# Second expert layer with the weights loaded and the hidden rows moving

## The chip, the cores and the metric

The kernel runs on one core of one Trainium2 chip. The metric is the device time of one execution in microseconds; lower is better. One further execution was profiled, and every row below comes from it.

## What is computed

Eight sequences of 2496 rows go through an attention without a softmax, and its 19968 result rows go through a mixture of eight experts. Each expert takes exactly 2496 rows, chosen greedily by the sorted gate logits.

```python
attn = np.maximum(scale * z @ z.T, 0.0) ** 2        # per sequence, z: 2496 x 64
x = (u * (attn @ v)).reshape(19968, 256)
# greedy by sorted logits x @ w_gate: token -> expert, 2496 rows each
for e in range(8):
    mask = assigned == e
    h = np.maximum(x[mask] @ w1[e], 0.0)            # 256 -> 1024
    out[mask] = h @ w2[e]                           # 1024 -> 256
```

All tensors are float32. Every float32 product is made of float32r parts: each operand is split into a high part (a copy rounded by ScalarE) and a low remainder (a subtraction on VectorE), and three products are summed: high by high, high by low, low by high.

## The kernel before

**Stages.** `attention` writes the rows x to a scratch tensor `xd` in HBM. `moe` then handles expert after expert (k), each in five groups (g) of rows: four of 512 and a last one of 448. A step n is one slice f of 128 of the 1024 hidden features of one group: 8 slices for a group, 40 steps for an expert, 320 in all. Beside the steps of one expert runs the routing of the next (`route`, a generator that `advance` drives in 88 units over 40 steps). It is a search for thresholds: VectorE makes masks (L124), TensorE counts them (L281, L405), VectorE picks the next interval, and at the end VectorE makes one-hot matrices (L523) which TensorE turns into row numbers (L529, L534).

**A group.** `gather_x` fetches 512 rows of `xd` by row number with four indirect DMAs of GpSimd's queue (L590). `tip_x` turns them on VectorE in blocks of 32 by 32 (L652), writes them with four DMAs of SyncE's queue to a scratch tensor `flat` (L655) and reads them back as features by rows (L658). `split_x` makes the high part on ScalarE (L665) and the low one on VectorE (L666). `layer1` multiplies w1 (loaded) by the turned rows (moving, six matmuls of 512 columns, L672 to L674), and makes the high part of the relu on ScalarE (L750) and the low part on VectorE (L752). In a group of 448 rows the low part of the last 64 rows goes to the free 64 columns of the high tile (L755).

**Second layer before.** For each of four blocks of 128 rows, `contract` loads the hidden block as weights and moves w2. The high and the low part of w2 lie side by side, so one matmul of 512 columns (L768) makes high by both, and one of 256 (L770) makes low by high. The last block of a group of 448 rows needs one matmul only (L765). Four PSUM banks, `y0` to `y3`, hold the result, already as rows. `put_y` adds the two halves (ScalarE copies one out, L792; VectorE adds the other, L793) and scatters the rows to the output with four indirect DMAs of GpSimd's queue (L801).

**Weights.** `load_w` loads an expert's w1 and w2 in four DMAs of SyncE's queue once the routing knows which expert comes next; `split_w` makes the two parts (ScalarE L618, VectorE L621). For w1 it reads every fourth element.

**Order.** A table (`at`) says at which step each part of a group is called, relative to the group's first step n0: gather at n0 - 12, `tip_x` at n0 - 8, `split_x` at n0 - 4, `put_y` at n0 + 7. `layer1` runs three steps ahead of `layer2`. Outside the parts that are written in a fixed order, a planner orders each engine's instructions by its own estimate of times; each engine then runs its list strictly in that order. `issue_after(x)` tells the planner that an instruction follows x on the same engine; `paced[-1]` is the low part (L752) made last. Of the eight PSUM banks, `hp` (result of layer 1) has two, `xp` and `srch` (routing) one each, `y0` to `y3` four.

Of the kernel before, what the change touches and what calls it, by code (L numbers as in the profile page):

```python
# [135 lines left out]
def moe(tc, xd, first, jp, identf, w1, w2, out, B, S, cp, dram):  # L136
# [18 lines left out]
    PLANS = ((4, 3, 3, 3, 3), (3, 3, 3, 3, 2, 2))  # L155
    ND = 15
    LA = 3
    AHEAD = 12
    LATE = 2
    YIELDS = 88  # L160
    with ExitStack() as ctx:
        rp = ctx.enter_context(tc.tile_pool(name="rp", bufs=1))
        wp = ctx.enter_context(tc.tile_pool(name="wp", bufs=3))
# [160 lines left out]
                with tc.issue_after(latest["mm"].ins):  # L324
                    nc.tensor.matmul(idle[:, :256], tri, oh[:, :32].rearrange("p j e -> p (j e)"), start=True, stop=True)  # L325

        paced = []

        def behind(lag):
            return tc.issue_after(paced[-lag].ins) if len(paced) >= lag else nullcontext()  # L330
# [253 lines left out]
        w1v = w1.rearrange("e (h p) (c f) -> e p c h f", c=2, p=128)  # L584
        w2v = w2.rearrange("e (c p q) d -> e p c q d", c=2, p=128)
        W1, W2, WR, XG, XT, XH, XL, HH, HL, HP, YP = {}, {}, {}, {}, {}, {}, {}, {}, {}, {}, {}
        scat = []

        def gather(dst, src, idx):
            return nc.gpsimd.indirect_dma_start(out=dst, out_offset=None, in_=src,  # L590
# [12 lines left out]
        def split_w(k, layer, c, half, parts="hl"):  # L603
            if half == 0 and "h" in parts:
                if layer == 1:
                    tiles = [wp.tile([128, 1024], F32R, name=f"w1{x}") for x in "hl"]
                    W1[k, c] = [t.rearrange("p (h q m) -> p h q m", h=DH, m=128) for t in tiles]
                else:
                    W2[k, c] = wp.tile([128, FT // 2, 2, D], F32R, name="w2")
            src = WR[k, layer, c]  # L610
            if layer == 1:
                src = src.rearrange("p (h m q) -> p h q m", h=DH, q=FT // 2)[:, half]
                h, l = [t[:, half] for t in W1[k, c]]
            else:
# [18 lines left out]
        def width(g):  # L633
            return min(512, S - 512 * g)

        def turn_x(k, g, ds):
            x = XG[k, g]
            w = width(g)
            t = [ps.tile([128, 512], F32, name=n, bufs=b) for n, b in (("xp", 1), ("hp", 2))]
            for d in ds:  # L640
                for i in range(4):
                    nc.tensor.transpose(t[d][:, i * 128:(i + 1) * 128], x[:, i, d * 128:(d + 1) * 128], identf)
            for d in ds:
                XH[k, g, d] = fp.tile([128, 512], F32R, name=f"xh{d}")[:, :w]
                XL[k, g, d] = fp.tile([128, 512], F32R, name=f"xl{d}")[:, :w]
                nc.scalar.activation(XH[k, g, d], t[d][:, :w], AF.Copy)
                nc.vector.tensor_sub(XL[k, g, d], t[d][:, :w], XH[k, g, d].bitcast(F32))

        def tip_x(k, g):
            tr = fp.tile([128, 2 * 4, 4, 32], F32, name="tr", bufs=1)  # L650
            with tc.issue_after(paced[-1].ins):
                nc.vector.transpose(tr.rearrange("p b t j -> p t b j"), XG[k, g].rearrange("p t d -> p (t d)"))  # L652
            flat = dram.tile([D, 512], F32, name="flat", bufs=2)
            for a in range(4):
                nc.sync.dma_start(flat[:, 128 * a:128 * a + 128].rearrange("(b i) n -> i b n", i=32),  # L655
                                  tr[32 * a:32 * a + 32].rearrange("i b t j -> i b (t j)"))
            XT[k, g] = fp.tile([128, DH, 512], F32, name="xt", bufs=1)
            nc.sync.dma_start(XT[k, g], flat.rearrange("(h p) n -> p h n", h=DH))  # L658

        def split_x(k, g):  # L660
            for d in range(DH):
                src = XT[k, g][:, d].rearrange("p (a t j) -> p t a j", a=4, t=4)
                hl = [fp.tile([128, 512], F32R, name=f"{n}{d}") for n in ("xh", "xl")]
                h, l = [t.rearrange("p (t a j) -> p t a j", t=4, a=4) for t in hl]
                nc.scalar.activation(h, src, AF.Copy)  # L665
                nc.vector.tensor_sub(l, src, h.bitcast(F32))  # L666
                XH[k, g, d], XL[k, g, d] = [t[:, :width(g)] for t in hl]

        def expand_part(k, g, f, p, c, d):
# [14 lines left out]
        def first_group():  # L684
# [11 lines left out]
            hp = [ps.tile([128, 512], F32, name=n, bufs=b) for n, b in (("hp", 2), ("hp", 2), ("y3", 1))]  # L696
# [43 lines left out]
        def layer1(k, g, f):  # L740
            w = width(g)
            if (k, g, f) in HP:
                p = HP.pop((k, g, f))
            else:
                p = ps.tile([128, 512], F32, name="hp", bufs=2)[:, :w]
                expand(k, g, f, p, slice(0, w))
            hh = fp.tile([128, 512], F32R, name="hh", bufs=LA + 1)
            h = hh[:, :w]
            l = fp.tile([128, 512], F32R, name="hl_", bufs=LA + 1)[:, :w]
            nc.scalar.activation(h, p, AF.Relu)  # L750
            n = w // 128 * 128
            paced.append(nc.vector.scalar_tensor_tensor(l[:, :n], p[:, :n], 0.0, h[:, :n].bitcast(F32),  # L752
                                                        op0=OP.max, op1=OP.subtract))
            if n < w:
                nc.vector.scalar_tensor_tensor(hh[:, w:w + w - n], p[:, n:], 0.0, h[:, n:].bitcast(F32),  # L755
                                               op0=OP.max, op1=OP.subtract)
            HH[k, g, f], HL[k, g, f] = hh, l
# [12 lines left out]
            nc.tensor.matmul(o[:, :D], l[:, c], w[:, 0], start=False, stop=(f == FT - 1), skip_group_check=True)  # L770

        def layer2(k, g, f):
            if f == 0:
                YP[k, g] = [ps.tile([128, 512], F32, name=f"y{i}", bufs=1) for i in range(4)]
            tail = FT - 1 - LA if (k, g) == (E - 1, NG - 1) else FT - 1
            if f < tail or tail == FT - 1:
                for i in range(4):
                    contract(k, g, f, i)
            elif f == FT - 1:
                for i in (3, 0, 1, 2):  # L780
                    for q in range(tail, FT):
                        contract(k, g, q, i)

        def put_y(k, g):
            y = fp.tile([128, 4, D], F32, name="y")
            idx = ROUTE[k]["idx"]
            w = width(g)
            order = (3, 0, 1, 2) if (k, g) == (E - 1, NG - 1) else range(4)
            for i in order:
                n = min(128, w - 128 * i)  # L790
                src = YP[k, g][i]
                nc.scalar.activation(y[:n, i], src[:n, D:], AF.Copy)  # L792
                nc.vector.tensor_add(y[:n, i], src[:n, :D], y[:n, i])  # L793
                if n < 128:
                    assert n == TL == 64
                    nc.vector.tensor_add(y[:n, i], src[TL:, :D], y[:n, i])
# [18 lines left out]
        for k in range(E):  # L815
            for g in range(NG):
                n0 = (k * NG + g) * FT
                if n0:
                    at(1 if (k, g) == (0, 1) else n0 - AHEAD + (LATE if (k, g) == (1, 0) else 0), gather_x, k, g)
                    if (k, g) == (0, 1):  # L820
                        at(n0 - 4, turn_x, k, g, range(DH))
                    else:
                        at(n0 - (7 if (k, g) == (1, 0) else 8), tip_x, k, g)
                        at(n0 - 4, split_x, k, g)
                at(n0 + FT - 1, put_y, k, g)
            n0 = k * PER
# [441 lines left out]
def _lay_out(inputs):  # L1268
# [16 lines left out]
    laid['moe_w1'] = _blocks(inputs['moe_w1'], 1)  # L1285
    return laid


# [20 lines left out]
```

## Time and profile before

| | us |
|---|---|
| median of 3 runs | 2434.04 (2432.58 to 2434.96) |
| time of the profiled execution | 2432.56 |
| its span, first to last instruction | 2430.5 |
| TensorE busy | 2380.0 |
| VectorE busy | 2068.5 |
| ScalarE busy | 1521.4 |
| GpSimd busy | 460.6 |
| mean granted clock of TensorE | 0.993 |

The span is 2.1 us shorter than the execution's time. Matmuls overlap in the records, so the distance from start to start tells their rate, and the duration does not. A granted clock of 1.0 is 2.4 GHz, 0.5 is 1.2 GHz; a stretch's figure is the mean. The attention ends at about 1370 us, the first expert's steps begin at about 1425 us, and the last routing ends at about 2200 us.

### The profile page before, as it was taken

Reading aid. Unit: us, or ns where it says so; the run is one execution under the profiler, and the core shown is the slowest. Engines: PE = TensorE matmul, PEld = TensorE weight load, DVE = VectorE, ACT = ScalarE, POOL = GpSimd, SP = SyncE. Lnnn points to the kernel's source line nnn. Section 1 sums busy time; section 2 is a strip of 40 time slices with the busy share of each in tenths; the row PEclk is TensorE's granted clock in tenths of the full one; section 3 lists DMA queues with packets and bytes.
Section 4 is the critical chain, followed back from the end, with each engine's and each line's share of the span. In section 5 each row is a group of like instructions: output and inputs, shape, how many; then the busy total and the mean of one; then the engine's idle time right before and its main releaser. Section 6 shows DMA issues by size and latency. Waiting matters only on the chain.

```text
span 2430.5 us, 42677 instructions
## 1 busy us (share of the span) xinstructions
PE 2380.0 (98%) x14724; PEld 1983.2 (82%) x14724; DVE 2068.5 (85%) x6220; ACT 1521.4 (63%) x2890; POOL 460.6 (19%) x690
## 2 busy tenths in 40 slices
PE   8999999999999999999999999899999999999998
PEld 6888888888888888888887787787888888888887
DVE  7898998998999998989989798979797979797443
ACT  7888888888888988888888223333332333333332
POOL 3020020020010200200100022333233333333332
PEclk9999999999999999999999999999999999999999
DMA  5153261261251532611511023232323323243331
GB/s 154 43 148 86 57 160 43 58 176 53 71 145 44 138 95 57 159 43 53 137 53 43 10 66 118 78 109 80 115 87 95 111 84 118 78 124 119 98 96 57
DMA packets 233848, 222.28 MB, mean 91 GB/s; under 512 B 95392, under 2 KB 192672, under 8 KB 233504
## 3 DMA queue, kind: packets, MB, share of 16 engines
q1 hardware_dynamic: 193088, 150.58, 21.3%
q0 software_dynamic: 40544, 68.98, 10.5%
q8 instruction: 116, 1.90, 0.3%
q14 instruction: 100, 0.82, 0.1%
HBM read 158.67 MB, written 60.82 MB: 90 GB/s over the span
## 4 chain that ended last, share of the span: by engine, by line
PE 82%; DVE 10%; issue 4%; POOL 1%; ACT 1%; DMA 1%; POOLq 0%; DVEq 0%; SPq 0%; ACTq 0%
PE acc L1038 41%; PE sc L996 11%; PE y L768 8%; PE hp L672 4%; PE hp L674 4%; PE hp L673 4%; PE y L770 4%; PE srch L281 2%; PE acc L1043 1%; POOL xg L590 1%; DVE mask L124 1%; DVE ob L523 1%; DVE w1l L621 1%; PE xp L325 1%; PE srch L529 1%
## 5 line engine op out<-in xcount | busy, mean ns | idle before, releaser
L1025 DVE TENSOR_TENSOR lo<-r,hi 128x512 fp32r<-128x512 f32 (+1 forms) x800 | 536.1, 673 | 83.1 <-ACT hi L1017 80.1
L1038 PE MATMUL acc<-hi,vh 128*128 128x512 f32 (+1 forms) x1520 | 590.8, 389 | 0.2 <-ACT vh L970 0.2
L1038 PE MATMUL acc<-lo,vh 128*128 128x512 f32 (+1 forms) x1520 | 587.7, 387 | 2.7 <-DVE lo L1025 2.7
L1038 PE MATMUL acc<-hi,vl 128*128 128x512 f32 (+1 forms) x1520 | 585.9, 385 | 0.0
L750 ACT ACTIVATE hh<-hp 128x512 fp32r<-128x512 f32 (+1 forms) x319 | 187.3, 587 | 629.9 <-PE hp L674 518.4
L1017 ACT ACTIVATE hi<-r 128x512 fp32r<-128x512 f32 (+1 forms) x780 | 500.2, 641 | 122.1 <-ACT r L1012 87.0
L1012 ACT ACTIVATE r<-r 128x512 f32<-128x512 f32 (+1 forms) x800 | 503.6, 639 | 2.5 <-DVE r L1006 2.4
L1079 DVE SCALAR_TENSOR_TENSOR lt<-xs,wgb 128x256 bf16<-128x256 f32 x1192 | 449.2, 417 | 0.0
L768 PE MATMUL y<-w,hh 128*128 128x512 f32 x1216 | 444.8, 399 | 0.7 <-DVE y L793 0.7
L1038 PEld LDWEIGHTS acc<-hi,vh 128*128 128x128 f32 x1520 | 286.2, 188 | 67.0 <-issue 13.8
L1008 ACT ACTIVATE r<-sc 128x512 f32<-128x512 f32 (+1 forms) x638 | 312.4, 614 | 40.3 <-PE sc L996 39.7
L1038 PEld LDWEIGHTS acc<-lo,vh 128*128 128x128 f32 x1520 | 286.3, 188 | 59.2 <-DVE lo L1025 8.2
L1038 PEld LDWEIGHTS acc<-hi,vl 128*128 128x128 f32 x1520 | 286.3, 188 | 52.1
L590 POOL DMA_INDIRECT xg<-xd,idx x160 | 181.2, 1133 | 513.3 <-DVE xg L628 281.1
L768 PEld LDWEIGHTS y<-w,hh 128*128 128x128 f32 x1216 | 229.0, 189 | 49.0 <-DVE y L793 2.2
L672 PE MATMUL hp<-xh,w1h 128*128 128x512 f32 (+2 forms) x642 | 256.5, 400 | 3.6 <-DVE hh L755 2.7
L673 PE MATMUL hp<-xl,w1h 128*128 128x512 f32 (+2 forms) x642 | 252.5, 393 | 1.2 <-DVE xl L666 1.1
L674 PE MATMUL hp<-xh,w1l 128*128 128x512 f32 (+2 forms) x642 | 250.6, 390 | 0.0
L996 PE MATMUL sc<-z,z 64*128 64x512 f32 (+1 forms) x1920 | 236.9, 389 | 4.2 <-ACT z L961 2.8
L996 PEld LDWEIGHTS sc<-z,z 64*128 64x128 f32 x1920 | 200.7, 185 | 31.2 <-ACT z L961 3.5
L959 POOL DMA_DIRECT2D z<-in_z_dram x35 | 18.7, 534 | 960.0 <-DVE lt L1079 530.0
L801 POOL DMA_INDIRECT out_dram<-y,idx x160 | 160.4, 1003 | 207.8 <-DVE y L793 120.9
(1193 smaller groups left out, 3152.1 us busy)
## 6 DMA issues: line engine op xcount, KB each, us to landing
ur<-in_u_dram SPq DMA_DIRECT2D x39, 512.0 KB
flat<-tr SPq DMA_DIRECT2D x152, 128.0 KB
xt<-flat SPq DMA_DIRECT2D x38, 512.0 KB
vh<-in_v_dram POOLq DMA_DIRECT2D x133, 128.0 KB
vr<-in_v_dram SPq DMA_DIRECT2D x32, 512.0 KB
xd<-tr SPq DMA_DIRECT2D x128, 128.0 KB
xs<-xd SPq DMA_DIRECT2D x32, 512.0 KB
wr<-in_moe_w_dram SPq DMA_DIRECT2D x32, 512.0 KB
```

The lines of the kernel that those rows point to most:

```text
L590: return nc.gpsimd.indirect_dma_start(out=dst, out_offset=None, in_=src, in_offset=bass.IndirectOffsetOnAxis(ap=idx, axis=0))
L672: nc.tensor.matmul(p[:, c], wh, xh, start=(d == 0), stop=False)
L673: nc.tensor.matmul(p[:, c], wh, xl, start=False, stop=False)
L674: latest["mm"] = nc.tensor.matmul(p[:, c], wl, xh, start=False, stop=(d == DH - 1))
L768: nc.tensor.matmul(o, h[:, c], w.rearrange("p s d -> p (s d)"), start=(f == 0), stop=(f == FT - 1), skip_group_check=True)
L996: nc.tensor.matmul(pair[s], key[b, p][r, c * 128:c * 128 + 128], query[b, g][r, :w], start=key is ZH and query is ZH, stop=key is ZL)
L1008: recent["r"] = nc.scalar.activation(r, p, AF.Relu, scale=scale)
L1012: nc.scalar.activation(R[n], R[n], AF.Square)
L1017: nc.scalar.activation(h, R[n], AF.Copy)
L1025: recent["l"] = nc.vector.tensor_sub(LO[n], a, h.bitcast(F32))
L1038: nc.tensor.matmul(o[d], w[:, c[d]], x, start=(kt == 0 and i == 0), stop=False)
L1079: nc.vector.scalar_tensor_tensor(t[r], src[r], 1.0, WG["rows"][r, e], op0=OP.mult, op1=OP.mult, accum_out=lg[r, j, e:e + 1])
```

## The change

The second layer exchanges its operands. w2 is loaded as weights and the hidden rows move, six matmuls of up to 512 columns for a slice (448 in a group of 448 rows). The result stands in two banks as features by rows, so it must be turned: VectorE turns each bank by blocks of 32 by 32 (`put_y`); three steps later `move_y` writes the blocks with four DMAs of SyncE's queue to a scratch tensor `rows` in HBM, in pieces of 64 floats, and reads them back as rows with one DMA (two in a group of 448); three more steps later `put_rows` scatters them. The very last group keeps the old way, with `xp` as one of its four banks.

The banks of the result rotate over three names (`YB`), and `hp` has three banks. Gather and `tip_x` come two steps sooner (`AHEAD` 14, `tip_x` at n0 - 10, `split_x` still at n0 - 4); since the routing's start is counted from `AHEAD`, it too starts and ends two steps sooner, except that `LATE` keeps expert 1's group 0 and the second start where they were. The turns of `tip_x` and `put_y` and the subtraction of `split_x` are collected in `before`, and the next L752 must follow them on VectorE. The low part of a 448-wide group is one instruction of 448 columns. Tiles `y` have one buffer instead of two, and so have the new tiles `yt`. On the host the columns of w1 are laid out so that `split_w` reads without a stride, and those of w2 so that the turned blocks give rows in order.

```diff
-    AHEAD = 12
-    LATE = 2
+    AHEAD = 14
+    LATE = 4
     YIELDS = 88
+    HPB = 3
+    YB = 3
...
             if layer == 1:
-                src = src.rearrange("p (h m q) -> p h q m", h=DH, q=FT // 2)[:, half]
+                src = src.rearrange("p (h q m) -> p h q m", h=DH, q=FT // 2)[:, half]
...
             with tc.issue_after(paced[-1].ins):
-                nc.vector.transpose(tr.rearrange("p b t j -> p t b j"), XG[k, g].rearrange("p t d -> p (t d)"))
+                before.append(nc.vector.transpose(tr.rearrange("p b t j -> p t b j"),
+                                                  XG[k, g].rearrange("p t d -> p (t d)")))
...
-                nc.vector.tensor_sub(l, src, h.bitcast(F32))
+                with tc.issue_after(paced[-1].ins):
+                    before.append(nc.vector.tensor_sub(l, src, h.bitcast(F32)))
...
-            n = w // 128 * 128
-            paced.append(nc.vector.scalar_tensor_tensor(l[:, :n], p[:, :n], 0.0, h[:, :n].bitcast(F32),
-                                                        op0=OP.max, op1=OP.subtract))
+            n = w // 128 * 128 if (k, g) == (E - 1, NG - 1) else w
+            with ExitStack() as turn:
+                while before:
+                    turn.enter_context(tc.issue_after(before.pop().ins))
+                paced.append(nc.vector.scalar_tensor_tensor(l[:, :n], p[:, :n], 0.0, h[:, :n].bitcast(F32),
+                                                            op0=OP.max, op1=OP.subtract))
...
         def layer2(k, g, f):
+            last = (k, g) == (E - 1, NG - 1)
             if f == 0:
-                YP[k, g] = [ps.tile([128, 512], F32, name=f"y{i}", bufs=1) for i in range(4)]
...
+                b = 2 * (k * NG + g)
+                names = [f"y{(b + d) % YB}" for d in range(DH)]
+                if last:
+                    names = names[:1] + ["xp"] + names[1:] + [f"y{(b + DH) % YB}"]
+                YP[k, g] = [ps.tile([128, 512], F32, name=n, bufs=1) for n in names]
+            if not last:
+                w = W2[k, f // 4][:, f % 4]
+                h, l = [t[k, g, f][:, :width(g)] for t in (HH, HL)]
+                for d in range(DH):
+                    c = slice(d * 128, d * 128 + 128)
+                    for i, (s, x) in enumerate(((0, h), (0, l), (1, h))):
+                        nc.tensor.matmul(YP[k, g][d][:, :width(g)], w[:, s, c], x, start=(f == 0 and i == 0),
+                                         stop=(f == FT - 1 and i == 2))
+                return
...
+            tr = fp.tile([128, 16, DH, 32], F32, name="yt", bufs=1)
+            with tc.issue_after(paced[-1].ins):
+                for d in range(DH):
+                    before.append(nc.vector.transpose(tr[:, :w // 32, d], YP[k, g][d][:, :w]))
+            YT[k, g] = tr
+
+        def move_y(k, g):
+            w = width(g)
+            tr = YT.pop((k, g))
+            rows = dram.tile([512, D], F32, name="rows", bufs=2)
+            dst = rows[:w].rearrange("(n i) d -> i n d", i=32)
+            for a in range(4):
+                nc.sync.dma_start(dst[:, :, 64 * a:64 * a + 64],
+                                  tr[32 * a:32 * a + 32, :w // 32].rearrange("i n h j -> i n (h j)"))
+            y = fp.tile([128, 4, D], F32, name="y", bufs=1)
+            n = w // 128
+            nc.sync.dma_start(y[:, :n], rows[:128 * n].rearrange("(t p) d -> p t d", p=128))
+            if n < 4:
+                nc.sync.dma_start(y[:w - 128 * n, n], rows[128 * n:w])
+            YT[k, g] = y
...
-                        at(n0 - (7 if (k, g) == (1, 0) else 8), tip_x, k, g)
+                        at(n0 - (7 if (k, g) == (1, 0) else 10), tip_x, k, g)
                         at(n0 - 4, split_x, k, g)
                 at(n0 + FT - 1, put_y, k, g)
+                if (k, g) != (E - 1, NG - 1):
+                    at(n0 + FT + 2, move_y, k, g)
+                    at(n0 + FT + 5, lambda k, g: put_rows(YT.pop((k, g)), k, g), k, g)
```

## Rows read from the trace of the kernel before

**Rows 1.** Busy time of each engine and its share of the span, from the page.

```profile
PE 2380.0 (98%) x14724; PEld 1983.2 (82%) x14724; DVE 2068.5 (85%) x6220; ACT 1521.4 (63%) x2890; POOL 460.6 (19%) x690
```

**Rows 2.** Stretches of the expert stage: length, busy per engine, clock, DMA share, GB/s.

```profile
1630.00:1680.00 50.00, 46.87 (x372) 39.55 (x371) 49.33 (x113) 19.11 (x35) 18.51 (x16) 1.00 0.37 120
1680.00:1756.00 76.00, 75.79 (x473) 62.56 (x473) 59.28 (x192) 22.81 (x45) 24.26 (x24) 0.98 0.29 83
1756.00:1806.00 50.00, 48.81 (x380) 41.35 (x380) 49.38 (x114) 19.66 (x35) 19.34 (x16) 1.00 0.39 124
...
2235.00:2415.00 180.00, 180.00 (x912) 153.11 (x910) 77.12 (x146) 59.43 (x118) 60.15 (x60) 1.00 0.30 88
```

**Rows 3.** TensorE's waits from 1500 to 2200 us: total, times, longest.

```profile
PE srch L281 <- DVE mask L124: 9.8, 5, 3.3
PE hp L672 <- DVE hh L755: 2.7, 1, 2.7
PE y L770 <- DVE hl__29448 L752: 2.0, 1, 2.0
PE srch L529 <- DVE ob L523: 1.9, 1, 1.9
```

**Rows 4.** TensorE's timeline, two blocks of 512-row groups: start, duration.

```profile
2264.58 0.39 PE L768 MATMUL y<-w,hh 128*128 128x512 f32 x1
...
2265.97 0.48 PE L672 MATMUL hp<-xh,w1h 128*128 128x512 f32 x1
...
2268.85 0.39 PE L672 MATMUL hp<-xh,w1h 128*128 128x512 f32 x1
...
2270.24 0.39 PE L768 MATMUL y<-w,hh 128*128 128x512 f32 x1
```

**Rows 5.** The same of the last 448-row group.

```profile
2405.64 0.37 PE L672 MATMUL hp<-xh,w1h 128*128 128x448 f32 x1
...
2406.86 0.39 PE L768 MATMUL y<-w,hh 128*128 128x512 f32 x1
...
2408.13 0.37 PE L672 MATMUL hp<-xh,w1h 128*128 128x448 f32 x1
```

**Rows 6.** VectorE's groups by line, 1600 to 2400 us: busy, mean ns of one.

```profile
L793 DVE TENSOR_TENSOR y<-y,y 128x256 f32<-128x256 f32 (+1 forms) x128 | 47.7, 415 | 0.0
...
L621 DVE TENSOR_TENSOR w1l<-wr,w1h 128x512 fp32r<-128x512 f32 x24 | 25.8, 1079 | 1.0 <-PE hp L674 1.0
...
L621 DVE TENSOR_TENSOR w<-wr,w 128x512 fp32r<-128x512 f32 x24 | 16.5, 690 | 0.6 <-ACT w L618 0.6
...
L755 DVE SCALAR_TENSOR_TENSOR hh<-hp,hh 128x64 fp32r<-128x64 f32 x48 | 10.2, 213 | 0.0
```

**Rows 7.** The attention's turn of a PSUM bank, group of the whole span by shape.

```profile
L1049 DVE STREAM_TRANSPOSE tr<-acc 128x512 f32<-128x512 f32 x64 | 41.8, 691 | 0.0
```

**Rows 8.** SyncE's queue in the attention: the turned rows written, then read back.

```profile
725.89 2.04 SPq L1062 DMA_DIRECT2D xd<-tr  x4
...
729.94 0.38 SPq L1066 DMA_DIRECT2D xs<-xd  x1
```

**Rows 9.** GpSimd's timeline, first and last scatter of one group, first of the last group.

```profile
2403.79 0.97 POOL L801 DMA_INDIRECT out_dram<-y,idx  x1 [17.16 <-DVE y L793]
...
2407.61 0.97 POOL L801 DMA_INDIRECT out_dram<-y,idx  x1 [0.30 <-issue]
2419.37 0.97 POOL L801 DMA_INDIRECT out_dram<-y,idx  x1 [10.78 <-DVE y L793]
```

**Rows 10.** ScalarE's timeline, first copies of the last group's result.

```profile
2417.78 0.85 ACT L792 ACTIVATE y<-y 64x256 f32<-64x256 f32 x2 [1.37 <-PE y L765]
```

**Rows 11.** GpSimd's timeline, the last issue of one gather.

```profile
2354.93 0.95 POOL L590 DMA_INDIRECT xg<-xd,idx  x1 [0.30 <-issue]
```

**Rows 12.** VectorE's timeline, the turn of that gather's rows.

```profile
2361.55 1.24 DVE L652 STREAM_TRANSPOSE tr<-xg 128x1024 f32<-128x1024 f32 x1
```

**Rows 13.** The chain that ended last, the longest landing of a gather on it.

```profile
1419.21 3.80 DMA xg<-xd,idx
```

More of the change, by code (lines that the diff above doesn't have):

```diff
@@ L325, in warm @@
                     nc.tensor.matmul(idle[:, :256], tri, oh[:, :32].rearrange("p j e -> p (j e)"), start=True, stop=True)
-        paced = []
+        paced, before = [], []
         def behind(lag):
@@ L586, in moe @@
         W1, W2, WR, XG, XT, XH, XL, HH, HL, HP, YP = {}, {}, {}, {}, {}, {}, {}, {}, {}, {}, {}
-        scat = []
+        YT, scat = {}, []
         def gather(dst, src, idx):
@@ L638, in turn_x @@
             w = width(g)
-            t = [ps.tile([128, 512], F32, name=n, bufs=b) for n, b in (("xp", 1), ("hp", 2))]
+            t = [ps.tile([128, 512], F32, name=n, bufs=b) for n, b in (("xp", 1), ("hp", HPB))]
             for d in ds:
@@ L695, in first_group @@
             turned = [ps.tile([128, 512], F32, name=f"y{c}", bufs=1) for c in range(2)]
-            hp = [ps.tile([128, 512], F32, name=n, bufs=b) for n, b in (("hp", 2), ("hp", 2), ("y3", 1))]
+            hp = [ps.tile([128, 512], F32, name="hp", bufs=HPB) for _ in range(3)]
             for d in range(DH):
@@ L744, in layer1 @@
             else:
-                p = ps.tile([128, 512], F32, name="hp", bufs=2)[:, :w]
+                p = ps.tile([128, 512], F32, name="hp", bufs=HPB)[:, :w]
                 expand(k, g, f, p, slice(0, w))
@@ L772, in layer2 @@
         def layer2(k, g, f):
+            last = (k, g) == (E - 1, NG - 1)
             if f == 0:
-                YP[k, g] = [ps.tile([128, 512], F32, name=f"y{i}", bufs=1) for i in range(4)]
-            tail = FT - 1 - LA if (k, g) == (E - 1, NG - 1) else FT - 1
-            if f < tail or tail == FT - 1:
+                b = 2 * (k * NG + g)
[12 more added lines that the diff above has]
+                return
+            tail = FT - 1 - LA
+            if f < tail:
                 for i in range(4):
@@ L784, in put_y @@
         def put_y(k, g):
-            y = fp.tile([128, 4, D], F32, name="y")
-            idx = ROUTE[k]["idx"]
[L787 to L796, printed above, removed]
+            w = width(g)
@@ new lines, in put_y @@
+            if (k, g) == (E - 1, NG - 1):
+                order = (3, 0, 1, 2)
+                y = fp.tile([128, 4, D], F32, name="y", bufs=1)
+                for i in order:
+                    n = min(128, w - 128 * i)
+                    o = y[:n, i].rearrange("p (a h j) -> p h a j", a=4, h=DH)
+                    h, l = [YP[k, g][i][:, c].rearrange("p (h a j) -> p h a j", a=4, h=DH)
+                            for c in (slice(0, D), slice(D, 2 * D))]
+                    nc.scalar.activation(o, l[:n], AF.Copy)
+                    nc.vector.tensor_add(o, h[:n], o)
+                    if n < 128:
+                        assert n == TL == 64
+                        nc.vector.tensor_add(o, h[TL:], o)
+                put_rows(y, k, g, order)
+                return
@@ new lines, in put_y @@
+            tr = fp.tile([128, 16, DH, 32], F32, name="yt", bufs=1)
[4 more added lines that the diff above has]
+        def move_y(k, g):
+            w = width(g)
+            tr = YT.pop((k, g))
[4 more added lines that the diff above has]
+                                  tr[32 * a:32 * a + 32, :w // 32].rearrange("i n h j -> i n (h j)"))
+            y = fp.tile([128, 4, D], F32, name="y", bufs=1)
+            n = w // 128
[3 more added lines that the diff above has]
+            YT[k, g] = y
@@ L797, in put_y, with put_rows @@
+        def put_rows(y, k, g, order=range(4)):
+            idx = ROUTE[k]["idx"]
             for i in order:
@@ L1284, in _lay_out @@
     laid['gate_rows'] = _blocks(inputs['moe_w_gate'].T, 1)
-    laid['moe_w1'] = _blocks(inputs['moe_w1'], 1)
+    w1, w2 = _blocks(inputs['moe_w1'], 1), inputs['moe_w2']
+    e, _, f = w1.shape
+    laid['moe_w1'] = w1.reshape(e, d, 2, 128, f // 256).swapaxes(3, 4).reshape(w1.shape)
+    laid['moe_w2'] = w2.reshape(e, f, 4, d // 128, 32).swapaxes(2, 3).reshape(w2.shape)
     return laid
```

## Prediction

> **What bounds the kernel now.** The page comes first: TensorE is busy in 98% of the span, VectorE in 85% [rows 1]. The change touches only the expert stage, so the view by stretches is next [rows 2]. Once the last routing has ended, TensorE is busy in all of 180 us and VectorE in 77 of them: matmuls alone set the pace there, whatever the others do. While a routing runs it is a mixture. In the 76 us stretches TensorE leaves 0.2 us idle and VectorE has room (59 of 76 us). In the 50 us stretches, which hold the one-hot matrices of one routing and the start of the next, VectorE is busy for 49.3 of 50 us, so it is the bound, and TensorE stands still for 1.2 to 3.1 us (two of five such stretches are shown). The view of TensorE's waits names the place [rows 3]: five waits of 9.8 us in sum before the routing's first count of an expert, for its mask, and three single waits of 6.6 us on VectorE's low parts and one-hot matrices, at the first and last routing. After two of these stalls the granted clock's mean over the next 76 us is 0.98 (1680 to 1756 us, and 2058 to 2134 us the same) [rows 2], a full 2.4 GHz for most of it and 1.2 GHz for a piece: 0.02 x 76 = 1.5 us each.
>
> So there are three sources of time: matmul work (all of the stage), VectorE's backlog (the 50 us stretches), the way out at the end.
>
> **Matmul work.** Start to start tells the rate. In a group of 512 rows the old second layer takes 2265.97 - 2264.58 = 1.39 us for its four pairs of 512 and 256 columns; the six matmuls of 512 columns of the first layer, which have the shape of the new second layer, take 2270.24 - 2268.85 = 1.39 us [rows 4]. The change saves nothing there; the rows are read to 0.01 us, which over 32 groups x 8 slices = 256 steps bounds it at 2.6 us either way. In a group of 448 rows the old layer takes 2408.13 - 2406.86 = 1.27 us (three pairs and one matmul), six of 448 columns take 2406.86 - 2405.64 = 1.22 us [rows 5]. That is 0.05 us in 8 slices of 7 groups (the last group keeps its form): -2.8 us. Term: **-2.8 us**, bounds -5.4 and 0.
>
> **VectorE's work.** Removed for a group: four additions of 0.415 us [rows 6]. Added: two turns of a PSUM bank, for which the attention has the same instruction at 0.691 us [rows 7]. That is 1.66 against 1.38 us. In a 448-row group eight L755 of 0.213 us go [rows 6], and each L752 grows by 64 columns (64/512 of 0.69 us, an estimate from w's row of 512 columns in rows 6, 0.09 us). Reading w1 with a stride costs 1.079 us for a half, w2's unstrided half 0.690 us [rows 6]; I take the latter for w1 after, four times for an expert. A 50 us stretch holds two results, two or three of the w1 halves and three L755: 0.56 + 0.78 + 0.38 = 1.7 us less, against a mean mask wait of 9.8 / 5 = 2.0 us. The order adds to it. The routing starts two steps sooner (two steps of 2.78 us), while `put_y` and `split_w` stay where they are, so a half of w2 (0.69 us), and perhaps one of w1, now falls behind the first mask instead of before it. Together 2.4 us or more, above the wait. But VectorE's list is made anew by the planner and tied by `before`, so I count 80% of the mask waits, 7.9 us, and half of the three single waits, 3.3 us, since less work helps there but nothing is moved. Term: **-11 us**, bounds 0 (the backlog stays) and -16.4.
>
> **Clock.** If the stalls go, so do the two drops behind them, 3.0 us. Term: **-2 us**, bounds -3 and 0.
>
> **What costs nothing.** ScalarE loses four copies a group; it is at 63% [rows 1] and waits for nobody that matters. The new turn must leave the first bank before the next group's second half needs it: after that bank's last matmul come three matmuls of the other bank, the next slice of layer 1 and three of the first half, 0.7 + 1.39 + 0.7 = 2.8 us by rows 4, and the turn takes 0.69 us; the old first bank had its three later pairs and layer 1, 2.4 us, for a copy and an addition. If VectorE's backlog passed 2 us there, TensorE would wait for the rest. Three `hp` banks loosen layer 1. The ties put L752 of a slice behind `put_y`'s two turns (1.4 us); its reader comes three steps later, so this is hidden unless a turn itself waits.
>
> **The way through HBM.** The attention does the same transfer: four writes issued in 2.04 us, the read back issued 4.05 us after the first write [rows 8]. For the read's landing I take the longest landing of a gather, 3.80 us [rows 13], as upper bound. A result is back 4.05 + 0.4 + 3.8 = 8.3 us after its turn, three steps; `put_rows` stands six steps behind `put_y`. The queues in a group's order (steps from n0): gather of the group after next at 2, `put_rows` of the group before at 5, `tip_x` of the group after next at 6, `move_y` at 10. On GpSimd's queue a late result would hold the next gather; it has three steps to spare. On SyncE's queue the rows stand behind `tip_x`, whose read back is over two steps earlier. DMA engines are at 0.29 to 0.39 [rows 2] and get 1 MB more for a group of 22 us; the attention moves as much for one of its groups. So zero in the middle.
>
> At the end it is on the path. The scatters of the last group but one start at 2403.79, right after its additions [rows 9]. In their place come the turns, then 8.3 us: about 2412. Four scatters follow at the old spacing (2407.61 - 2403.79 = 3.82 us for three steps, so 1.27 us each): the last is issued near 2417 and lands at most 3.8 us later, 2421. `y` now has one buffer, so ScalarE's first copy for the last group, at 2417.78 before [rows 10], waits until then; its four scatters run back to back and move by as much. Upper bound 3 us, lower 0 (a quick landing), taken +1.5. Term: **+1.5 us**.
>
> The Trainium skill (DMA: Bandwidth & Descriptors, Specifications) speaks against the change here: pieces under 512 B are read, modified and written, and the new rows go out in pieces of 256 B. The attention's writes are of the same size and need the 4.05 us above all in all, which shows no such penalty. By the rule, taken as a doubling of the time between the last write and the read (from 2.0 to 4.0 us), the end would cost +3.5 instead of +1.5 and the time be 2 us more.
>
> **Sum.** -2.8 - 11 - 2 + 1.5 = -14.3 us. The profiled execution took 2432.56 us, which is 1.5 us under the median; the median after is 2434.04 - 14.3, about **2419 us**.
>
> **Rivals.** What this kernel's measurement can tell from no change is about 0.2%, 4.9 us: faster is below 2429.2, slower above 2438.9.
>
> A, the forecast: part of VectorE's backlog goes. Own range 2411 to 2428. Chance 0.54.
>
> B, the backlog stays. For it: the planner orders by its own estimates, and waits that rest on a difference between estimate and chip come back elsewhere; 1.7 us of relief is less than the mean wait. Then -2.8 + 1.5: 2433 us. Chance 0.18.
>
> C, all goes. -5.4 - 16.4 - 3, and some 3 us of small waits beside those shown, end at 0: 2406 us. For it: VectorE's share in the 50 us stretches would fall from 99% to about 95%. Chance 0.14.
>
> D, slower: the ties make VectorE stand. `tip_x`'s turn waits for its gather, and now L752 may not pass it. Before, 2361.55 - 2355.88 = 5.7 us lie between the last issue of a gather and the turn [rows 11, 12], and a landing takes up to 3.8 us [rows 13], so 1.9 us are spare, and then two steps (5.6 us) before TensorE needs the L752 behind it. It decides if gathers come over 7.5 us later than now, behind a scatter that waits for its result on GpSimd's queue, or because the gathers of 1 KB rows share the engines with the added pieces. From there each 0.3 us costs 0.3 us at each of some 31 turns, 9 us: 2442 us. Against it: the three steps above. Chance 0.10.
>
> The remaining 0.04 is a cost that I do not see.
>
> Faster: nearly all of A, C, a little of B, 0.71; same: most of B and the edge of A, 0.17; slower: D and the rest, 0.12. The range leaves out D's time and the better half of C: 2404 to 2435.
>
> **What will show it.** Right: TensorE's second layer at six matmuls 0.23 us apart, 0.20 in 448-row groups; no L793 but the last group's; the turn near 0.69 us; w1's low half near 0.69 us; the waits for L124 below 2 us in sum; no clock drop near 1690 and 2069 us. Wrong: VectorE still at 99% in the 50 us stretches with the mask waits as long as before (B); VectorE idle before the turn of `tip_x`, released by a gather's landing (D); the second layer's spacing above 0.24 us, which would cost 256 x 6 x 0.01 = 15 us for each 0.01; at the end, ScalarE's first copy of the last group released by a scatter's landing, and by how much after 2417.8 less what was gained.

## The result, and the profile after

The changed kernel takes 2465.31 us (median of 4 runs, 2460.79 to 2468.79) against 2434.11 us: 1.0128 of the time before, 95% interval 1.0110 to 1.0145. That is 31 us slower, where 15 us faster was forecast, and outside the range. The profiled execution has a span of 2462.8 us at a mean granted clock of 0.986 (before 2430.5 us at 0.993).

The page's line of busy times answers to [rows 1].

```profile
PE 2376.5 (96%) x14156; PEld 1962.8 (80%) x14156; DVE 2041.3 (83%) x6079; ACT 1457.9 (59%) x2734; POOL 458.1 (19%) x690
```

TensorE has less work (2376.5 us, though part of it ran at half clock) in a longer span. The view by stretches shows where it stands, with the columns of [rows 2]; the stretches are cut by time, and the slower kernel has not quite the same work in them:

```profile
1500.00:1630.00 130.00, 108.96 (x693) 86.57 (x691) 99.83 (x277) 29.32 (x51) 42.23 (x34) 0.93 0.40 114
1630.00:1680.00 50.00, 49.61 (x365) 40.23 (x366) 45.64 (x109) 13.24 (x23) 12.68 (x11) 0.97 0.47 140
1680.00:1756.00 76.00, 71.38 (x395) 57.74 (x394) 58.13 (x175) 20.10 (x35) 24.75 (x25) 0.96 0.46 126
1756.00:1806.00 50.00, 48.74 (x368) 39.00 (x367) 44.92 (x106) 12.69 (x22) 14.27 (x14) 1.00 0.54 160
...
2235.00:2415.00 180.00, 175.50 (x836) 145.83 (x837) 81.26 (x129) 47.52 (x83) 64.00 (x64) 0.98 0.48 134
```

VectorE is no longer busy for the whole of a 50 us stretch, as if its backlog had gone. Yet TensorE now stands even in the last 180 us, where no routing runs, and 4.6 us of the 76 us stretch, where it had 0.2 us idle before (0.4 to 1.1 us in the three other stretches of that length). Neither engine is the bound: both wait. TensorE's waits from 1500 to 2200 us (total, times, longest) name the place, beside [rows 3]:

```profile
PE srch L407 <- DVE hx L291: 17.1, 9, 4.6
PE srch L283 <- DVE mask L124: 11.9, 10, 3.3
```

The mask waits are as large in sum as before, in other places. New is the first row: TensorE stands at the search's second matmul (L407) for `hx`, the end of a short chain on VectorE behind the count (L283, `hd` L288, `hr` L290, `hx` L291). One of these places, in the timelines of GpSimd, TensorE, VectorE and ScalarE:

```profile
1458.35 0.95 POOL L592 DMA_INDIRECT xg<-xd,idx  x1 [13.56 <-DVE xg L630]
...
1462.13 0.96 POOL L592 DMA_INDIRECT xg<-xd,idx  x1 [0.30 <-issue]
1463.40 1.01 POOL L849 DMA_INDIRECT out_dram<-y,idx  x1 [0.31 <-issue]
...
1467.28 0.97 POOL L849 DMA_INDIRECT out_dram<-y,idx  x1 [0.30 <-issue]
```

```profile
1465.35 0.42 PE L283 MATMUL srch<-mask,oh 128*128 128x48 bf16 x10 [0.91 <-DVE Dg L417]
...
1467.54 0.39 PE L793 MATMUL y<-hl__19870,w 128*128 128x512 f32 x1
1471.65 0.37 PE L407 MATMUL srch<-hx,onesr 128*128 128x32 f32 x1 [3.72 <-DVE hx L291]
```

```profile
1469.89 0.21 DVE L288 TENSOR_TENSOR hd<-srch,diag 128x48 f32<-128x48 f32 x1 [3.92 <-remote]
...
1469.97 0.60 ACT L754 ACTIVATE hh<-hp 128x512 fp32r<-128x512 f32 x1 [5.24 <-remote]
```

The count ended at 1465.77, and the next `hp` (L678) at 1467.48 by the same timeline. VectorE was idle, yet `hd` began 4.1 us after the count; ScalarE began 2.5 us after L678, at the same moment. "Remote" is a releaser that the view can't name. The trace also records the updates of TensorE's semaphore: the three that are due at the ends of matmuls at 1465.78, 1467.48 and 1467.93 us are recorded at 1469.86, 1469.95 and 1469.99 us, while in a quiet place (e12, 1600 to 1604 us) each follows its matmul within 0.02 us. So it is the signals that come late. Both engines stood until 1.6 us after the end of a row of eight indirect transfers on GpSimd's queue: four gathers and four scatters with 0.3 us between them. Counting the places from 1425 us on where `hd`, `best` or layer 1's relu begins over 0.5 us after its matmul has ended with its own engine free ("late places"): 3 with 4.2 us in all before, 41 with 80 us after (missing matmul records make some of them). Rows of eight (under 0.7 us between transfers): 3 before, 19 after.

Why do gather and scatter now meet? SyncE's and GpSimd's timelines of one group. VectorE's two turns of its result ended at 2209.3 us.

```profile
2216.38 3.09 SPq L834 DMA_DIRECT2D rows<-yt  x4
2227.69 0.80 SPq L658 DMA_DIRECT2D flat<-tr  x2
2228.81 0.38 SPq L838 DMA_DIRECT2D y<-rows  x1
2229.24 1.03 SPq L658 DMA_DIRECT2D flat<-tr  x2
```

```profile
2239.94 1.28 POOL L592 DMA_INDIRECT xg<-xd,idx  x1 [19.33 <-DVE xg L630]
2241.52 1.08 POOL L849 DMA_INDIRECT out_dram<-y,idx  x1 [0.30 <-issue]
...
2245.47 1.33 POOL L849 DMA_INDIRECT out_dram<-y,idx  x1 [0.30 <-issue]
2247.10 0.99 POOL L592 DMA_INDIRECT xg<-xd,idx  x1 [0.30 <-issue]
```

The planner put the read back (L838) among the four pieces of the next turned rows (L658). These wait for their gather and turn, so the read is issued 9 us after the last write's issue, where 2.3 us are enough in the last group (below). The scatter starts 32 us after the turn, in the midst of a gather. Over the expert stage GpSimd waits 342 us for results (27 waits; before, 120.9 us for `put_y`'s additions):

```profile
POOL out_dram L849 <- DMA y<-rows: 342.1, 27, 33.5
```

Matmuls went the other way, better than forecast. Blocks of six in TensorE's timeline, of 512 columns (beside [rows 4]), then of 448 (beside [rows 5]):

```profile
2291.35 0.39 PE L793 MATMUL y<-hh,w 128*128 128x512 f32 x1
...
2292.71 0.39 PE L676 MATMUL hp<-xh,w1h 128*128 128x512 f32 x1
...
2294.07 0.39 PE L793 MATMUL y<-hh,w 128*128 128x512 f32 x1
...
2331.18 0.36 PE L793 MATMUL y<-hh,w 128*128 128x448 f32 x1
...
2332.39 0.37 PE L676 MATMUL hp<-xh,w1h 128*128 128x448 f32 x1
...
2333.61 0.36 PE L793 MATMUL y<-hh,w 128*128 128x448 f32 x1
```

A step takes 2.72 us against 2.78, and 2.43 against 2.49 in a 448-row group.

The account, from 1425 us on: some -19 us of matmuls (worked out below); +38 us of standing (gaps of over 0.6 us between the starts of two matmuls, each less 0.23 us: 60.7 us in sum, 22.9 before); +19 us of clock (51.2 us at 1.2 GHz against 13.7, half of the difference); +2.5 us at the end. That makes 40 us; the span grew by 32.3. A gap at the low clock is counted twice, which explains about 5 us of the difference (10.3 us of the gaps lie in pieces at 1.2 GHz, 1.1 before); the rest is not explained.

### The profile page after: what moved, and what is told of

It is laid out like the page before. It is cut to its first block, busy times and chain, and to the rows that moved or that the text cites. A ratio compares the mean times of both kernels' runs of the same rounds, so it can differ in the third digit from the quotient of the medians.

```text
span 2462.8 us, 41367 instructions
## 1 busy us (share of the span) xinstructions
PE 2376.5 (96%) x14156; PEld 1962.8 (80%) x14156; DVE 2041.3 (83%) x6079; ACT 1457.9 (59%) x2734; POOL 458.1 (19%) x690
## 5 line engine op out<-in xcount | busy, mean ns | idle before, releaser
L793 PE MATMUL y<-hh,w 128*128 128x512 f32 (+1 forms) x1248 | 448.2, 397 | 6.4 <-DVE yt L825 5.7
L793 PEld LDWEIGHTS y<-hh,w 128*128 128x128 f32 x1248 | 238.4, 191 | 51.2 <-DVE yt L825 7.4
L678 PE MATMUL hp<-xh,w1l 128*128 128x512 f32 (+2 forms) x646 | 253.2, 392 | 0.0
L849 POOL DMA_INDIRECT out_dram<-y,idx x160 | 173.3, 1083 | 402.8 <-DMA y<-rows 342.1
L592 POOL DMA_INDIRECT xg<-xd,idx x160 | 165.5, 1034 | 357.2 <-DVE xg L630 175.1
```

What stands on the lines that cost most here:

```text
L678: latest["mm"] = nc.tensor.matmul(p[:, c], wl, xh, start=False, stop=(d == DH - 1))
L793: nc.tensor.matmul(YP[k, g][d][:, :width(g)], w[:, s, c], x, start=(f == 0 and i == 0), stop=(f == FT - 1 and i == 2))
L849: st = nc.gpsimd.indirect_dma_start(out=out, out_offset=bass.IndirectOffsetOnAxis(ap=idx[:n, a:a + 1], axis=0), in_=y[:n, i], in_offset=None)
```

## The experiments

The theories. T1: the two round trips share SyncE's in-order list, the result comes late, GpSimd waits for it. T1b, what T1 leads to: gather and scatter meet in rows of eight, and TensorE's signals reach the other engines late. T2: the ties hold VectorE. T3: the moved steps (gather, turn). T4: the added traffic itself. Ratios are to the kernel before, with 95% intervals.

**Ties and steps.** e1 leaves out the ties, e2 puts the steps back.

```
-    before.append(nc.vector.transpose(...))      # e1, also split_x and put_y
+    nc.vector.transpose(...)
-    AHEAD = 14; LATE = 4; ... else 10), tip_x    # e2
+    AHEAD = 12; LATE = 2; ... else 8), tip_x
```

> The changed kernel without the orders that the change wrote into VectorE's list (a layer's second output is no longer placed behind the turns and remainders of its step); everything else as changed (2465 us). T1, the result's read back stands behind the next turned transfer on SyncE and the scatter that waits for it crowds the gather: no help, 2455 to 2475 us, GpSimd's wait for the result still near 340 us in all. T2, the ties make VectorE stand: back to 2440 us or less, and the waits for the hx and the mask fall by over half. T3 (steps of gather and turn) and T4 (the added traffic) expect what T1 expects.

> The changed kernel with the gather 12 steps ahead, the first one 2 steps late and the turn of rows 8 steps ahead, as before the change (14, 4 and 10 in the change). T3, the moved steps are the cause: 2440 us or less. T1: the turn and its transfer come two steps later, so the read back still falls behind them on SyncE, 2450 to 2475 us, and GpSimd's wait for the result stays over 250 us. T4: no change, 2460 to 2470.

Measured: e1 2461.2 us, 1.0117 [1.0100, 1.0134], so the ties are not the cause (T2 falls). e2 2488.75 us, 1.0234 [1.0214, 1.0253]: worse, so the moved steps help here (T3 falls). The time is above every range given. GpSimd's wait for results is not the 250 us expected of T1 but 77 us: with the gather later, the waiting moves to the gathers (301 us, 175 in the changed kernel), and there are 24 rows of eight.

**The trip and its traffic.** e3 scatters straight from the turned tile (two buffers, no trip; it leaves out putting the rows back in order). e7 adds the same transfers to e3 with nobody waiting for them.

```
-    rows = dram.tile(...); four writes; y = fp.tile(...); read back    # move_y, e3
-    YT[k, g] = y
+    YT[k, g] = tr.rearrange("p (i a) h j -> p i (a h j)", i=4)
+    rows = dram.tile(...); four writes; back = dram.tile(...); back <- rows    # e7 on e3
```

> The changed kernel without the result's way through HBM: the turned result is scattered straight from the turned tile, which has two buffers (the rows come out in a wrong order, and the half tile is taken from the tile before it). T1 and T4, the transfers are the cause: the gain of the matmul work comes through, 2405 to 2425 us, GpSimd's wait for the result under 60 us in all, PE's signals late in fewer than 6 places. T2 and T3: 2450 us or more, the ties and steps being as changed.

> The kernel without the trip (2410 us; rows scattered straight from the turned tile, in a wrong order) with the trip's transfers put back on SyncE as idle traffic: the same four writes of 256-byte pieces, and the same bytes copied back from the rows to another place in HBM; no scatter waits for them. T4, traffic itself: 2450 us or more. T1, the scatter's wait for the result: 2405 to 2425 us. In between (2425 to 2450): SyncE's list, in which the turned rows now stand behind the result's pieces, has a share of its own.

Measured: e3 2410.14 us, 0.9913 [0.9897, 0.9930]; e7 2414.88 us, 0.9925 [0.9908, 0.9942]. Traffic and SyncE's fuller list cost 3 us by the ratios, 5 by the times (T4 falls as the main cause); the rest hangs on somebody's waiting for the result. e3 has 7 late places. Its scatters still wait 197.6 us for the turn, not the under 60 us expected: a wait on GpSimd need not cost anything by itself.

**Where the trip is issued.** e4 puts the read back ahead of the next turned rows on SyncE; e5 keeps the two trips in strict turn; e6 issues the result's trip from ScalarE; e10 is e6 with the read back three steps after the writes; e13 issues only the read back from GpSimd.

```
+    with tc.issue_after(came[-1].ins):         # e4: four flat pieces behind the latest read back
+        [nc.sync.dma_start(flat[...], ...) for a in range(4)]
+    # e5: also the four rows pieces behind the latest read of xt
-    nc.sync.dma_start(...)                     # move_y, all: e6; the read back alone: e13
+    nc.scalar.dma_start(...)                   # e6
+    nc.gpsimd.dma_start(y[:, :n], ...)         # e13
+    at(n0 + FT + 5, back_y, k, g)              # e10: read back, behind that step's relu
```

> The changed kernel with one order added on SyncE: the four pieces of the next turned rows come behind the latest read of a result, so that no read back stands behind a turn. Transfers, ties and steps as changed. T1: most of the loss goes, 2415 to 2440 us, scatters are released 8 us earlier and GpSimd's wait for the result halves. T4, traffic: no change, 2460 to 2470 us. T2 and T3: no change.

> The changed kernel with SyncE's list in strict turn: pieces of the turned rows, their read back, pieces of the result, its read back, so that neither round trip is split by a wait of the other. With only the result's read back put ahead the time had stayed at 2465 us. T1, the two trips wait for one another in one in-order list: 2420 to 2445 us. T1b, what costs is that gather and scatter come back to back on GpSimd and TensorE's signals are then late, whatever SyncE's order: 2455 to 2470 us with 15 or more late places. T4, traffic: 2455 to 2470.

> The changed kernel with the result's writes and read back issued by ScalarE instead of SyncE; sizes, pieces and order otherwise as changed. T1: SyncE's waits can no longer hold the result, 2415 to 2440 us, if ScalarE does not itself stand on the landing of the rows (then PE waits for ScalarE's relu, above 2460 us). T4, traffic: 2455 to 2475.

> The kernel with the result's trip on ScalarE's queue (2440 us) with the read back issued three steps after the writes, behind the relu of its step, and the scatter one step later, so that ScalarE does not stand on the landing of the rows (30 us of such waits there). T1: ScalarE's waits for the rows fall under 5 us and the time to 2420 to 2432 us, if no scatter falls behind the next gather; scatters 17 us after the turn. If ScalarE's eight DMA issues a group themselves are the cost: 2436 us or more.

> The changed kernel with the result's read back issued by GpSimd, just ahead of the scatter that needs it, instead of SyncE; the writes stay on SyncE. T1: no read back behind a turn on SyncE and nobody due behind GpSimd's wait, so scatters 10 to 14 us after the result's turn instead of 17 to 28, gather and scatter apart, 2415 to 2430 us. T4, traffic, or a GpSimd queue that is now the late one: 2450 us or more.

Measured: e4 2465.03 us, 1.0132 [1.0113, 1.0151]; e5 2516.38 us, 1.0328 [1.0301, 1.0354]; e6 2440.36 us, 1.0034 [1.0021, 1.0046]; e10 2433.94 us, 1.0008 [0.9999, 1.0018]; e13 2410.43 us, 0.9904 [0.9888, 0.9921]. T1's forecast for e4 and e5 failed: whichever trip goes first on SyncE, the other stands behind it. In e4 GpSimd's wait for results falls to 226 us, but the turned rows come late instead (TensorE waits 8.4 us for `xl`), and 14 rows of eight are left. In e5 the pieces of the result stand behind the read of the turned rows, and TensorE waits 35.3 us in 19 places for the result's next turn (that `yt` has one buffer may be why), beside 10.8 us for `xl`. Off SyncE the loss goes: in part with the trip on ScalarE (e6 0.4 us above its range, with 30.1 us of ScalarE standing on the rows' landing; e10 2 us above its range, and with 32.5 us of this wait where under 5 had been expected, so its gain over e6 has another reason), and wholly with the read back on GpSimd. e13 beats both kernels and its own range. GpSimd's timeline there, for a 448-row group:

```profile
1952.51 0.95 POOL L592 DMA_INDIRECT xg<-xd,idx  x1 [0.30 <-issue]
1953.46 0.81 POOL L838 DMA_DIRECT2D y<-rows  x1
...
1959.07 1.02 POOL L849 DMA_INDIRECT out_dram<-y,idx  x1 [4.21 <-DMA y<-rows]
```

The read back itself stands between gather and scatter and parts them by 5.6 us. One row of eight and 2 late places are left.

**The row of eight by itself.** e8 is e3 with each scatter put behind the latest gather, so that eight transfers run in a row. e12 is e8 with three iotas on a spare tile between them.

```
+    with tc.issue_after(took[-1].ins): st = nc.gpsimd.indirect_dma_start(...)     # e8
+    for _ in range(3):                                                            # e12, before the scatters
+        nap = nc.gpsimd.iota(scratch, pattern=[[1, 256]], base=0, ...)
```

> The kernel without the trip (2410 us) with each scatter put behind the gather of two groups on, so that eight indirect transfers run back to back on GpSimd; no other transfer added. T1b, back-to-back gather and scatter delay TensorE's signals and with them the routing's chain: 2430 us or more, 15 or more late places, PE's waits for hx and mask several times the 8.4 us of the kernel without the trip. If the late signals come only with the trip's traffic: 2405 to 2420 us and fewer than 8 late places.

> The kernel with eight indirect transfers back to back (no trip, 2452 us) with some 4.5 us of other work for GpSimd (three iotas of 1.5 us on a tile that nobody reads) between each gather and the scatter behind it; order of all lists as there. T1b, it is the unbroken row of eight that delays TensorE's signals: 2405 to 2425 us and fewer than 8 late places, although the scatter comes later. If the order alone costs (gathers kept from their place, rows late): 2445 us or more.

Measured: e8 2451.8 us, 1.0078 [1.0059, 1.0097]; e12 2398.02 us, 0.9855 [0.9838, 0.9871]. The instruction lists of TensorE, VectorE, ScalarE and SyncE are the same in e3, e8 and e12, instruction for instruction; only GpSimd's differs. Rows of eight or more: 6 in e3, 35 in e8, 1 in e12; late places 7, 34 and 4. VectorE's waits ahead of `hd` in e8 from 1420 us on, then TensorE's for `hx`:

```profile
DVE hd L288 <- PE hp L678: 24.6, 8, 4.1
DVE hd L288 <- PE srch L283: 14.0, 23, 2.4
DVE hd L288 <- remote: 11.3, 3, 4.8
```

```profile
PE srch L407 <- DVE hx L291: 24.7, 11, 4.8
```

The same two in e12, and the pause in GpSimd's timeline:

```profile
DVE hd L288 <- PE srch L283: 8.5, 20, 0.8
```

```profile
PE srch L407 <- DVE hx L291: 1.8, 1, 1.8
```

```profile
1901.08 0.95 POOL L592 DMA_INDIRECT xg<-xd,idx  x1 [0.30 <-issue]
1902.05 1.19 POOL L842 IOTA scratch<- 128x256 bf16 x3
1904.64 1.01 POOL L845 DMA_INDIRECT out_dram<-yt,idx  x1 [1.40 <-issue]
```

Work added to GpSimd and a later scatter make the kernel 54 us faster, and 12 us faster than e3, more than expected. The three iotas take 1.2 us together (4.5 us had been expected from a longer iota); with the issue behind them the two rows of four stand 2.6 us apart.

**The same pause in both kernels.** What stayed open was how much of the changed kernel's own loss is the row of eight, and how much the late result as such. e14 puts the three iotas between all neighbouring fours of the changed kernel, e15 of the kernel before, e16 of e13.

```
+    nap()     # ahead of each four gathers and each four scatters, order of GpSimd's list kept by issue_after
```

> The changed kernel with three short iotas (1.2 us together, on a tile that nobody reads) on GpSimd between every four gathers and the four scatters beside them; the read back stays on SyncE behind the turn, the scatters stay as late as they are. T1b, the unbroken row of eight is what costs: 2415 to 2430 us, no row of eight, fewer than 8 late places, although GpSimd's wait for the result stays above 250 us. If half of the loss comes from late gathers and rows themselves: 2435 to 2450 us. If the pause does nothing here: 2460 us.

> The kernel before with the same pauses. It has three rows of eight against 19 in the changed kernel and three late places of 4.2 us in all, so T1b gives 2428 to 2434 us. If the pauses help in another way than by parting rows of eight (a longer interval for anything else): 2415 us or less.

> The changed kernel with the read back on GpSimd ahead of its scatter (2410 us) and the same pauses. It has one row of eight left, so T1b gives no change, 2405 to 2412 us; under 2400 if rows of four still cost.

Measured: e14 2421.24 us, 0.9969 [0.9959, 0.9980]; e15 2429.26 us, 1.0000 [0.9990, 1.0009]; e16 2408.00 us, 0.9913 [0.9896, 0.9929]. The other four engines' lists are the same in e14 as in the changed kernel, and in e15 as before. In e14 the result is still late, but no row of eight and no late place is left, and the time is 44 us less than the changed kernel's (39 us by the two ratios: the kernel before was also faster beside e14, 2429.29 us). GpSimd's wait, TensorE's two waits (1500 to 2200 us), and VectorE's for `hd`:

```profile
POOL out_dram L862 <- DMA y<-rows: 292.1, 30, 23.1
```

```profile
PE srch L283 <- DVE mask L124: 12.1, 10, 2.9
...
PE srch L407 <- DVE hx L291: 2.9, 2, 1.8
```

```profile
DVE hd L288 <- PE srch L283: 10.4, 25, 1.1
```

GpSimd still waits 292 us, and the `hx` waits fall from 17.1 to 2.9 us. The pause changes nothing where there are hardly any rows of eight (e15, e16), so its gain goes with these rows.

## Why the prediction was wrong

**The step that failed** is "The way through HBM": "zero in the middle". It read the queues in the order in which the program calls them, and so found the result back "8.3 us after its turn" and three steps to spare on GpSimd's queue. The planner's list for SyncE has the read back among the pieces of the next turned rows, and the scatter shown started 32 us after the turn. That alone costs less: e14, with the result as late, takes 2421 us. The larger price came from what the late scatter then met: the next gather. Parting the rows of eight gives back 39 to 44 us, a cost for which the forecast had no term. Three rows of eight and 4.2 us of late places were in the trace before, and they were not read.

**Matmul work**, -2.8 us: right in sign, too small. The forecast held the first layer at 1.39 us for six matmuls and the second equal to it. Once all matmuls of a step are of one width, both layers take 1.36 us. That makes 256 steps x 0.06 = 15.4 us, and 56 steps of 448 rows x 0.06 = 3.4 us, some -19 us, read to 0.01 us a block. Over the whole stage, at full clock, the median of a first-layer block of 512 columns is 1.39 us before (184 blocks) and 1.36 us after (175).

**VectorE's backlog**, -11 us: hardly came in the changed kernel, but its mechanism was right. The durations were (turn 0.695 us, w1's half 0.682 us). TensorE's waits for the mask from 1600 to 2180 us (total, times, longest), before, in e13 and in e14:

```profile
PE srch L281 <- DVE mask L124: 9.1, 4, 3.3
```

```profile
PE srch L283 <- DVE mask L124: 0.2, 1, 0.2
```

```profile
PE srch L283 <- DVE mask L124: 7.2, 7, 2.9
```

In the changed kernel they are 7.3 us in seven places, in e12 there are none. So where the rows are on time the four waits behind VectorE's list go. In e14, 4.7 of the 7.2 us are two waits (1692 and 1941 us) behind a turn of `tip_x` for which VectorE itself stood (below, rival D). VectorE's share of the 50 us stretches does not fall, as rival C had it, but TensorE's idle time there does, in e14 beside [rows 2]:

```profile
1630.00:1680.00 50.00, 50.00 (x372) 42.21 (x371) 49.45 (x109) 15.54 (x28) 23.15 (x25) 1.00 0.57 163
...
1756.00:1806.00 50.00, 49.51 (x376) 41.47 (x375) 49.34 (x112) 14.70 (x26) 19.92 (x28) 1.00 0.50 133
```

The standing comes back elsewhere, in terms that the forecast did not have or put at nothing. Around the second expert's start (1500 to 1630 us) TensorE's waits of over 0.6 us make 6.3 us before, 12.4 in e14 and 14.3 in e13, of which 6.6 us are one wait behind a turn of `tip_x`. And at 2196 us of e14 it waits 4.1 us for the turn of a bank that the next group needs, which "What costs nothing" had named and put at nothing.

So e14's 2421 us, near the forecast, is no proof of its sum; it is near by luck. By the account used above it is -19 us of matmuls, +7 of standing (29.8 us of gaps), +2 of clock (17.1 us at 1.2 GHz) and +3 at the end: -7, where the ratio gives 7.5 us (0.0031 x 2434) and the two spans differ by 11. By its size rival B was nearer for the changed kernel, by the mechanism A was. The 45 of 50 us in the changed kernel is VectorE waiting, not relief.

**Clock**, -2 us: the sign turned. The stalls brought pieces at 1.2 GHz: the mean over 1500 to 1630 us is 0.93 (before 0.97), and over 1680 to 1756 us 0.96 against 0.98 [rows 2]. In e13 and e14 the two drops that were named do not come: 1.00 over 1680 to 1756 and over 2058 to 2134 us.

**The end**, +1.5 us: right in kind, near the upper bound. From the end of the last matmul to the end of the span it takes 12.0 us against 9.5, so +2.5. The sign named came: ScalarE's first copy of the last group is released by a scatter's landing.

```profile
2450.25 0.65 ACT L815 ACTIVATE y<-y 64x256 f32<-64x256 f32 x2 [4.14 <-DMA out_dram<-y,idx]
```

There, with nothing else on SyncE, the trip went as costed:

```profile
2434.65 2.20 SPq L834 DMA_DIRECT2D rows<-yt  x4
2439.19 0.38 SPq L838 DMA_DIRECT2D y<-rows  x1
...
2443.86 0.97 POOL L849 DMA_INDIRECT out_dram<-y,idx  x1 [9.50 <-DMA y<-rows]
```

The read follows the first write by 4.54 us (the attention: 4.05 us [rows 8]) and the scatter by 9.2 us, against 8.3 us costed. The Trainium skill's rule on pieces under 512 B (DMA: Bandwidth & Descriptors, Specifications), taken as an estimate that doubles the time behind the last write, gave 6.05 us for the first; the measured 4.54 us is nearer to the attention's value.

**Rival D** had the right place, a gather behind a scatter that waits for its result on GpSimd's queue, and a chance of only 0.10. Its mechanism, VectorE standing on the turn of the next rows, was not what cost here: in the changed kernel VectorE stands over 0.5 us before none of these turns, and without the ties the time stays (e1). Its sign does come in e14, 17.7 us in eleven places, most of it released by a gather's landing:

```profile
DVE tr L664 <- DMA xg<-xd,idx: 13.4, 7, 3.0
```

and once in e13 (5.5 us at 1549 us).

What stays open: e14 is still 11 us above e13 (16 by the ratios), and e13 12 us above e12. VectorE's standing on late gathers in e14 (4.7 us of mask waits) and the traffic (3 to 5 us by e7) are likely parts; they were not separated further. Each run's span and clock come from the profiler's records, so no run shows how late the signals would be with nothing recorded.

## What to carry to other kernels

A step in the program is not a place in a queue: where a planner orders the lists, read for each new transfer which waiting instruction it will stand behind, and who stands behind it. Put round trips that wait on different things on different in-order queues (e6: 25 us less than the change as it was made), or issue the read back on the queue of its only reader (e13: 55 us less). When an engine's timeline shows long rows of indirect transfers, look for signals that arrive late elsewhere before believing the engine that seems to wait.

## What was not expected of the hardware

Eight indirect transfers in a row on GpSimd, 0.3 us apart, go with completions of TensorE that reach ScalarE and VectorE up to 4.9 us late, mostly in the second half of the row; ScalarE and VectorE are then released together. In rows of four it was about 1 us in e3 and up to 1.7 us in e7. A gap of some 2.3 to 2.6 us between fours, filled by three iotas, removes it: e12 against e8 -54 us, e14 against the changed kernel -39 to -44 us, with no other engine's list changed. A gap of 0.9 to 1.0 us does not: in the changed kernel two such places (1761 and 1861 us) have signals 1.4 and 2.6 us late. How a queue of transfers holds up another engine's signal, whether the time or the iota is what helps, and where between 1.0 and 2.3 us the bound lies, was not tried.

The rows leave a second mark. From 1425 us on the trace of the kernel before lacks 53 of the 771 updates that TensorE's matmuls make to its semaphore, that of the changed kernel 56 of 664; up to 1425 us, with four gathers in all, none of 1806 and none of 1809 is missing, and in e14, e15 and e16, with iotas ahead of every four, none either. This loss by itself costs no time that shows (e15: 1.0000).

The second surprise is the matmul rate: the first layer's matmuls, unchanged, come 0.227 us apart when all are 512 columns wide, against 0.232 us in the mix with 256-column ones. That the mix is the reason was not tried by itself.
